# Step 0 of a gated attention: two tiles' keys on GpSimd, two pairs' masks on ScalarE and GpSimd, new places for the later steps

## The chip, the cores and the metric

The kernel runs on one core of one Trainium2 chip. The metric is the device time of one execution in microseconds. Three runs of the kernel before took 467.12, 467.70 and 467.71 us, so the median is 467.7 us.

## What is computed

A gated linear attention over 4 sequences of 768 steps with 8 heads of 48 channels, and then a two-layer network on its output:

```python
f = sigmoid(f_logit)
for t in range(768):
    state = f[t][:, None] * state + outer(k[t], v[t])      # per sequence and head, 48x48
    y[t] = q[t] @ state
h = y @ w_in                                               # 384 -> 2048
g = where(h >= 1, h, where(h <= -1, 0, (h + 1) ** 2 / 4))
out = g @ w_out                                            # 2048 -> 384
```

The large products run in a reduced format with a high and a low part for each operand, three products for each.

## The kernel before

**Steps and units.** Time is cut into six steps of 128. The attention of a step is made by blocks: the gates' running products scale keys and queries, keys times queries give a block of scores, a triangular mask cuts it, and the masked scores times the values give the step's output. From step 1 on the state of the steps before is added. The network of a step is 16 units (96 in all). A unit is 9 matrix products of 512 columns into `ph` (L317, for unit 0 L960), an activation of five instructions on ScalarE and VectorE (L320, L323, L328, L331, L334), and 9 products of 512 columns into `po` (L341).

**Step 0.** The heads lie in three tiles of 128 partitions (`m` = 0, 1, 2). `gate(m)` makes one tile's keys and queries: a sigmoid on ScalarE (L542, L544), a backward scan into `w` on VectorE (L546, s1), a copy of its ends by GpSimd (L550), a reciprocal (L552, rc), a forward scan (L553, s2), then keys times `w` (L556, km) and queries times the second scan (L558, qm). All of these after the sigmoid are on VectorE except L550 and two tiny GpSimd instructions (L563, L565). Tiles 0 and 2 go in two halves of two sequences. The scans' second operands are the constant tiles `least_w` and `rec` in SBUF. `w` is one buffer: the next tile's first scan waits until the keys of the tile before have read it.

TensorE then makes scores of four pairs of heads (L638 for pairs 0, 1 and 2, L668 for the last pair, which is put together from slices of all three tiles, so that it is complete only after tile 2). Eight masks (L681, `masks`) multiply a score bank by the mask on VectorE. `heads` (L917) and `thirds` (L932) make step 0's output from the masked scores, `rounded` (L761, L762) splits it in a high and a low part, and unit 0 begins.

**The order.** `Plan` holds every instruction group with an engine, a cost from the table `COST` and what it depends on. A list scheduler fixes each engine's order before the kernel is built; on the chip each engine works through its queue in that order and waits on semaphores. TensorE's groups stay in the order in which they are added: `START` gives it for step 0; `TURNS` and `VISITS` say beside which unit the later steps' transposes and attention stand (for each pair of pairs four places: scores, state sums, begin, output; several at one place make one stretch of TensorE's work). Where the scheduler expects a gap on TensorE in the first 20 us it puts products of zeros there (L396). `LOOK` names the engines on which the scheduler lets an instruction wait for a much more urgent one that is nearly ready.

Of the kernel before, what the change touches and what calls it, by code (L numbers as in the profile page):

```python
# [19 lines left out]
ALU = mybir.AluOpType  # L20
PSUM = bass.MemoryType.PSUM

B, H, S, D = 4, 8, 768, 48
C = 128
# [28 lines left out]
LATENCY = dict(PE=235, ACT=140, DVE=110, POOL=150)  # L53
COST = dict(mm=227, narrow=120, scores=1000, scores_half=500, heads=960, thirds=1020, half=330, both=940, begin=430, before=880, part=450, states=700, before_half=440, parts=730, parts_last=730, zeros=4000, turn=395, first=160, last=200,
            rows=316, turned_rows=150, scan=1140, dve=602, small=200, sums=467, gate=600, act=575, bits=660, round=485, copy=520, turned=412, sig=538, decay=226,
            issue=480, near=600, least=300)


INSTRUCTIONS = dict(scores=32, scores_half=16, heads=32, thirds=32, both=128, begin=64, before=128, before_half=64, part=64, states=64, parts=128, parts_last=64, zeros=24, turn=8)
BLOCK, FIRST_BLOCK, AHEAD, BEHIND, FETCH, OFFSET, WAITS = 256, 193, 48, 40, 3700, 9, 1.0045  # L60


LOOK, MARGIN, GAP = ("ACT", "DVE"), 100, 3000

SOONER = 2000
GATHER_BEHIND, GATHER_LATER = (0, 0, 0), 6000

TURNS = {4: 6.5, 6: 9.5, 8: 15.5, 10: 22.5, 12: 25.5, 14: 41.0, 16: 44.0, 18: 52.0, 20: 60.0, 22: 69.0}
VISITS = {4: (8.0, 8.0, 11.0, 11.0), 6: (11.0, 12.5, 12.5, 12.5), 8: (21.0, 21.0, 22.0, 22.0), 10: (25.0, 25.0, 28.5, 28.5), 12: (28.5, 34, 36.0, 36.0), 14: (36.0, 42.5, 42.5, 42.5), 16: (49.0, 49.0, 55.0, 55.0), 18: (54.0, 55.0, 57.0, 57.0), 20: (66.0, 66.0, 75.0, 75.0), 22: (75.0, 77, 77, 77)}
HOMES = [(k + 3) % 5 for k in range(25)]  # L70
START = (("scores", 0), ("mask", 0, 0), ("mask", 0, 1), ("last", 0), ("scores", 1), ("mask", 1, 0), ("mask", 1, 1), ("last", 1),
         ("scores", 2, 0), ("last", 2, 0), ("scores", 2, 1), ("last", 2, 1), ("first", 0), ("first", 1),
         ("mask", 2, 1), ("mask", 3, 1), ("mask", 2, 0), ("mask", 3, 0), ("second", 0), ("second", 1), ("second", 2), ("second", 3))
AFTER = {1: (('turn', 0), ('turn', 1), ('turn', 2)), 4.5: (('states', 0), ('states', 2)), 2: (('turn', 3),)}

# [23 lines left out]
class Plan:  # L99
# [7 lines left out]
    def add(self, engine, cost, emit, *deps, kb=0, count=None):  # L107
        flat, made = [], count is not None

        def spread(d):  # L110
            if isinstance(d, list):
                for e in d:
                    spread(e)
            elif d is not None and d not in flat:
                flat.append(d)

        spread(list(deps))
        cost, kind = COST[cost] if isinstance(cost, str) else cost, cost
        count = count or INSTRUCTIONS.get(kind) or 2 * max(1, round(cost / (COST["mm"] if cost % COST["mm"] == 0 else COST["narrow"])))
        if engine == "PE":  # L120
            if self.tensor is not None and self.tensor not in flat:
                flat.append(self.tensor)
            small = made or kind in SMALL_PRODUCTS
            cost += (COST["last"] if small else COST["first"]) if small != self.small else 0
            self.small = small
        o = Op(engine, cost, emit, flat, kb)
        if engine == "PE":
            o.count = count
        for d in flat:
            d.users.append(o)  # L130
        if engine == "PE":
            self.tensor = o
        self.ops.append(o)
        return o
# [96 lines left out]
def gla_moe(ctx: ExitStack, tc: tile.TileContext, ff, kqd, f0, vv, vad, vbd, wd, fixedd, gates, values, headsd, out):  # L231
    nc = tc.nc
# [46 lines left out]
    def wide(a):  # L279
        return a.rearrange("r b c -> r (b c)")  # L280
# [70 lines left out]
    add = plan.add  # L351

    def dma(dst, src, kb, *deps):
        return add("SP", "issue", lambda: nc.sync.dma_start(dst, src), *deps, kb=kb)
# [4 lines left out]
    def vec(cost, fn, *deps):  # L359
        return add("DVE", cost, fn, *deps)  # L360

    def sca(cost, fn, *deps):
        return add("ACT", cost, fn, *deps)
# [7 lines left out]
    def fresh(t):  # L371
        nc.gpsimd.memset(t, 0.0)

    def start_least():
        nc.vector.memset(least_w, 1e-30)
        nc.vector.memset(least_w[:, :, 0], 1.0)


    set_kq = add("POOL", 1500, lambda: nc.gpsimd.memset(kq[NP - 1], 0.0))
    set_least = vec(400, start_least)  # L380
    set_rec = add("POOL", 800, lambda: fresh(rec))
    set_ds = add("POOL", 200, lambda: fresh(ds[0][:, 2 * B * D:]))

# [126 lines left out]
    def old(n, *names, of=att):  # L510

        return [] if n < 0 else [of[n].get(k) for k in names]

    def gate(m):

        i, p = divmod(m, NT)
        t = kq[p]

        ft, before = (f[m], None) if m < 2 else (act_f[1], None) if m == 2 else (f[(m - 1) % 2], m - 3 if m < 5 else m - 2)
        et = end[m % 2]  # L520
        steps = ((0, 2), (2, 4)) if m in (0, 2) else ((0, 4),)
        count = len(steps)
        c = gates_of[m] = {k: [] for k in ("km", "qm", "sg", "en", "s1", "s2")}
        lk = c["lk"] = dma(t[:, 0:2 * N], kqd[i, p], 512, old(NP * (i - 1) + p, "sc", "y", "tr"),
                           old(m - NT, "km", "qm", "to", of=gates_of))
        if m == 0:
            ready["mask"] = ready["mask_t"] = ready["ident"] = dma(fixed, fixedd, 160)
            ready["f0"] = sca(200, lambda: nc.scalar.activation(f0s[:, 0:NI * NT * B], f0s[:, 0:NI * NT * B], AF.Sigmoid), dma(f0s, f0, 36))
        for h, (b0, b1) in enumerate(steps):
            cols = slice(b0 * C + (1 if b0 else 0), b1 * C + 1)  # L530
            if m != 2:
                l = dma(ft[:, cols], ff[i, p, :, cols], 256 // count, gates_of[before]["qm"] if before is not None else None)
            elif h == 0:
                l = dma(ft[:, 0:N + 1], ff[i, p, :, 0:N + 1], 256)
                l.early = SOONER
            last = old(m - 1, "km", "en", "s2", of=gates_of)
            u0, u1 = B - b1, B - b0
            fwd = ft[:, b0 * C:b1 * C]
            bwd = ft[:, b1 * C:b0 * C:-1]
            kt, qt = wide(part(t, 0)[:, u0:u1]), wide(part(t, 1)[:, b0:b1])  # L540
            if m != 2:
                sg = sca("sig" if count == 1 else 308, lambda cols=cols: nc.scalar.activation(ft[:, cols], ft[:, cols], AF.Sigmoid), l)  # L542
            elif h == 0:
                sg = sca("sig", lambda: nc.scalar.activation(ft[:, 0:N + 1], ft[:, 0:N + 1], AF.Sigmoid), l)  # L544

            s1 = vec(COST["scan"] if count == 1 else 602, lambda bwd=bwd, u0=u0, u1=u1: nc.vector.tensor_tensor_scan(  # L546
                out=wide(w[:, u0:u1]), data0=bwd, data1=wide(least_w[:, u0:u1]), initial=0.0,
                op0=ALU.mult, op1=ALU.max), sg, c["sg"], set_least, last)
            last_w = w[:, u1 - 1:(u0 - 1 if u0 else None):-1, C - 1]
            en = add("POOL", "least", lambda b0=b0, b1=b1, last_w=last_w: nc.gpsimd.tensor_copy(  # L550
                out=et[:, b0:b1], in_=last_w), s1, old(m - 2, "pf", of=gates_of))
            rc = vec("small", lambda b0=b0, b1=b1, last_w=last_w: nc.vector.reciprocal(out=rec[:, b0:b1, 0], in_=last_w), s1, last, set_rec)  # L552
            s2 = vec(COST["scan"] if count == 1 else 602, lambda fwd=fwd, b0=b0, b1=b1: nc.vector.tensor_tensor_scan(  # L553
                out=fwd, data0=fwd, data1=wide(rec[:, b0:b1]), initial=0.0, op0=ALU.mult, op1=ALU.add), rc, s1, c["s1"])
            c["s1"].append(s1)
            km = vec(COST["gate"] if count == 1 else 335, lambda kt=kt, u0=u0, u1=u1: nc.vector.tensor_tensor(  # L556
                out=kt, in0=kt, in1=wide(w[:, u0:u1]), op=ALU.mult), s1, lk)
            qm = vec(COST["gate"] if count == 1 else 335, lambda qt=qt, fwd=fwd: nc.vector.tensor_tensor(  # L558
                out=qt, in0=qt, in1=fwd, op=ALU.mult), s2, lk)
            for name, d in (("sg", sg), ("en", en), ("km", km), ("qm", qm), ("s2", s2)):  # L560
                c[name].append(d)
        to, f0m = whole(t), f0s[:, m * B:m * B + B]
        o = add("POOL", "least", lambda: nc.gpsimd.tensor_tensor(out=to, in0=et, in1=f0m, op=ALU.mult),  # L563
                c["en"], ready["f0"], c["lk"], old(NP * (i - 1) + p, "db"))
        c["pf"] = [o, add("POOL", "least", lambda: nc.gpsimd.tensor_copy(out=f0m, in_=to), o)]  # L565

    va = sd[:, 0:4 * B * 64].rearrange("u (b h e) -> u b h e", b=B, h=4)
    vb = v_all[:, 0:B * 384].rearrange("u (b e) -> u b e", b=B)
# [105 lines left out]
    def masks(n, h):  # L674

        c = att[n]
        c.setdefault("am", [None, None])
        b, ps, _ = c["held"][h]
        t = am_of[n][h]
        free = {(2, 0): lambda: att[0]["ys"][0], (3, 0): lambda: att[0]["ys"][1], (3, 1): lambda: att[3]["pt"][1]}.get((n, h), lambda: None)  # L680
        o = vec("dve", lambda: nc.vector.tensor_tensor(  # L681
            out=t, in0=ps, in1=mask.rearrange("u (o t) -> u o t", o=1).broadcast_to([C, B, C]), op=ALU.mult),
            c["sc"], ready["mask"], free())
        banks[b][:] = [o]
        c["am"][h] = o
# [628 lines left out]
```

## Time and profile before

| | us |
|---|---|
| median of three runs | 467.7 |
| span of the profiled execution, first to last instruction | 465.4 |
| what lies around that span, against the median | 2.3 |
| TensorE busy in the span | 460.2 |
| VectorE / ScalarE / GpSimd busy | 368.9 / 268.5 / 25.3 |
| start of unit 0 on TensorE | 23.18 |
| end of the last product | 461.28 |

The page gives the span of the profiled execution and no separate time for it; the table sets the span beside the median. Busy matrix products overlap and their ends are modelled, so starts of matmuls are the safer reading: in the steady part they lie 0.227 us apart.

### The profile page before, as it was taken

The page shows a single profiled execution, that of the slowest core. Times are in us where ns is not written, and L with a number is a line of the kernel's source. Part 1 is how long each engine was busy: PE and PEld are TensorE (multiplying, and loading weights), DVE is VectorE, ACT ScalarE, POOL GpSimd, SP SyncE. Part 2 cuts the span into 40 slices and gives each one's busy share as a digit, 9 for nine tenths or more (in the row PEclk, how much of TensorE's full clock was granted, in tenths as well). Part 3 has the DMA queues.
Part 4 walks back from the last instruction along what each step waited for, and adds up shares of the span by engine and source line. Part 5 has one row for each costly group of instructions (what it writes and reads, how often), then busy time and mean ns, then how long its engine had stood idle before and what let it go on. Part 6 is the DMA issues. An engine that isn't in the chain of part 4 may idle for free.

```text
span 465.4 us, 10974 instructions
## 1 busy us (share of the span) xinstructions
PE 460.2 (99%) x4551; PEld 378.2 (81%) x4551; DVE 368.9 (79%) x709; ACT 268.5 (58%) x502; POOL 25.3 (5%) x67
## 2 busy tenths in 40 slices
PE   9999999999999999999999999999999999999996
PEld 4888888888888888888888888888888888888885
DVE  7999998899999999888889987867665565655633
ACT  4599999765565646546547344556445544554443
POOL 4100110000002000002001000000000000000000
PEclk9999999999999999999999999999999999999999
DMA  8897855271050252031424016603402323434101
GB/s 293 324 330 279 296 177 170 78 216 51 3 159 1 54 130 85 28 116 48 127 56 125 25 47 200 174 2 75 142 1 86 98 78 94 159 104 123 45 0 72
DMA packets 20308, 54.35 MB, mean 117 GB/s; under 512 B 3328, under 2 KB 3968, under 8 KB 20256
## 3 DMA queue, kind: packets, MB, share of 16 engines
q1 hardware_dynamic: 20256, 53.63, 36.7%
q8 instruction: 36, 0.59, 0.5%
q14 instruction: 16, 0.13, 0.1%
HBM read 44.77 MB, written 4.72 MB: 106 GB/s over the span
## 4 chain that ended last, share of the span: by engine, by line
PE 99%; DVE 0%; ACT 0%; issue 0%; DVEq 0%
PE po L341 43%; PE ph L317 42%; PE pa L777 2%; PE ph L396 2%; PE pa L808 2%; PE ph L716 2%; PE pa L884 1%; PE pa L742 1%; PE ph L668 1%; PE ph L960 0%; PE pa L716 0%; PE pa L932 0%; PE pa L917 0%; PE po L638 0%; PE pa L863 0%; PE ph L884 0%
## 5 line engine op out<-in xcount | busy, mean ns | idle before, releaser
L317 PE MATMUL ph<-x,w_hi 128*128 128x512 f32 x570 | 145.4, 391 | 0.0
L320 ACT ACTIVATE act<-ph,half 128x512 f32<-128x512 f32 x96 | 66.0, 687 | 108.6 <-PE ph L317 108.3
L317 PEld LDWEIGHTS ph<-x,w_hi 128*128 128x128 f32 x570 | 106.6, 188 | 22.2
L328 DVE SCALAR_TENSOR_TENSOR act<-ph,act 128x512 f32<-128x512 f32 x96 | 66.1, 688 | 44.3 <-ACT act L323 43.2
L331 ACT CAST ghi<-act 128x512 fp32r<-128x512 f32 x96 | 59.5, 620 | 60.8 <-DVE act L328 60.4
L341 PE MATMUL po<-ghi,w_hi 128*128 128x512 f32 x287 | 84.3, 396 | 0.0
L341 PE MATMUL po<-ghi,w_lo 128*128 128x512 f32 x287 | 82.6, 390 | 0.0
L341 PE MATMUL po<-glo,w_hi 128*128 128x512 f32 x287 | 82.6, 390 | 0.0
L334 DVE TENSOR_TENSOR glo<-act,ghi 128x512 fp32r<-128x512 f32 x96 | 66.2, 689 | 18.5 <-ACT ghi L331 16.1
L317 PE MATMUL ph<-x,w_lo 128*128 128x512 f32 x285 | 80.1, 389 | 0.0
L756 DVE STREAM_TRANSPOSE kn<-kq 32x128 f32<-32x128 f32 x224 | 67.8, 303 | 3.6
L341 PEld LDWEIGHTS po<-ghi,w_lo 128*128 128x128 f32 x287 | 53.9, 188 | 11.4
L341 PEld LDWEIGHTS po<-glo,w_hi 128*128 128x128 f32 x287 | 53.9, 188 | 11.3
L317 PEld LDWEIGHTS ph<-x,w_lo 128*128 128x128 f32 x285 | 53.5, 188 | 11.2
L323 ACT ACTIVATE act<-act 128x512 f32<-128x512 f32 x96 | 60.7, 632 | 2.7
L341 PEld LDWEIGHTS po<-ghi,w_hi 128*128 128x128 f32 x287 | 52.7, 188 | 10.9
L469 DVE TENSOR_REDUCE ok<-raw 128x1 f32<-128x512 f32 x48 | 31.4, 680 | 13.6 <-DMA raw<-in_w 13.6
L550 POOL COPY end<-w 128x4 f32<-128x4 f32 (+1 forms) x20 | 7.1, 357 | 282.9 <-DVE w L546 242.9
L546 DVE TENSOR_TENSOR_SCAN w<-f,least_w 128x512 f32<-128x512 f32 (+1 forms) x18 | 20.7, 1157 | 2.0 <-ACT f L542 2.0
L553 DVE TENSOR_TENSOR_SCAN f<-f,rec 128x512 f32<-128x512 f32 (+1 forms) x18 | 20.7, 1156 | 0.1
L457 DVE TENSOR_TENSOR w_lo<-bits,w_hi 128x512 fp32r<-128x512 f32 (+1 forms) x25 | 16.1, 662 | 0.2
L456 ACT CAST w_hi<-bits 128x512 fp32r<-128x512 f32 (+1 forms) x25 | 14.5, 598 | 0.8 <-DVE bits L452 0.8
(138 smaller groups left out, 396.2 us busy)
## 6 DMA issues: line engine op xcount, KB each, us to landing
kq<-in_kq SPq DMA_DIRECT2D x18, 512.0 KB, 4.4
raw<-in_w SPq DMA_DIRECT2D x18, 512.0 KB, 3.6
raw<-in_w SPq DMA_DIRECT2D x14, 511.6 KB, 5.2
out_y<-raw SPq DMA_DIRECT2D x17, 256.0 KB, 2.5
f<-in_f SPq DMA_DIRECT2D x16, 256.5 KB, 2.9
v<-in_v SPq DMA_DIRECT2D x10, 384.0 KB, 4.6
raw_late<-in_w SPq DMA_DIRECT2D x7, 511.6 KB, 4.8
raw<-in_w SPq DMA_DIRECT2D x12, 256.0 KB, 3.8
```

The costliest lines, as they stand in the source:

```text
L317: nc.tensor.matmul(ps[:, to], w_in(w_hi if high else w_lo, j, kt), xt[:, kt, t, c], start=(n == 0), stop=(n == 8))
L320: nc.scalar.activation(a, ps, AF.Relu, bias=half, scale=0.5)
L323: nc.scalar.activation(a, a, AF.Square)
L328: nc.vector.scalar_tensor_tensor(out=a, in0=ps, scalar=1.0, in1=a, op0=ALU.max, op1=ALU.min)
L331: nc.scalar.copy(hi, a)
L334: nc.vector.tensor_tensor(out=lo, in0=a, in1=hi.bitcast(F32), op=ALU.subtract)
L341: nc.tensor.matmul(po[e][:, c], w_out(part, j, e), g[:, of], start=(j == 0 and n == 0 and c.start == 0), stop=(j == NJ - 1 and n == 2))
L457: l = vec(COST["dve"] * n // W, lambda: nc.vector.tensor_tensor(out=lo, in0=whole_val, in1=hi.bitcast(F32), op=ALU.subtract), h)
L469: seen.append(vec("dve", lambda z=z, op=op: nc.vector.tensor_reduce(out=ok[:, 1 + NG + z + c:2 + NG + z + c], in_=words_of(raw[2])[1].bitc ...
L546: s1 = vec(COST["scan"] if count == 1 else 602, lambda bwd=bwd, u0=u0, u1=u1: nc.vector.tensor_tensor_scan(out=wide(w[:, u0:u1]), data0=bw ...
L553: s2 = vec(COST["scan"] if count == 1 else 602, lambda fwd=fwd, b0=b0, b1=b1: nc.vector.tensor_tensor_scan(out=fwd, data0=fwd, data1=wide( ...
L756: nc.vector.transpose(kn[n % 2][u:u + 32, ::-1, r:r + 32], src[:, :, u:u + 32])
```

## The change

In step 0 alone:

- For tiles 0 and 1 the scans' second operands lie in two PSUM banks (`early`), which VectorE fills at the start by three more memsets. Tile 2 and the later steps keep `least_w` and `rec` in SBUF.
- For tiles 0 and 1 the keys' product (L556) is done by GpSimd. The first scan of tile 1 waits for the keys of tile 0 as before (they are now on another engine), and by a new dependency for tile 0's queries too.
- The four masks of pairs 0 and 1 are a copy of the score bank to SBUF by ScalarE and then an `affine_select` in place by GpSimd, in place of one VectorE product each. The four masks of pairs 2 and 3 stay on VectorE.
- `START` puts the first `heads` group between the two halves of tile 2's scores.
- `LOOK` takes in GpSimd, and four costs are set: `least`, `pf`, `select`, `keys`.
- `TURNS` and `VISITS` are new. 16 different places of attention stand in `VISITS` where there were 17: the scores (54), state sums (55) of the second half of step 4 and the output of its first half (55) come together at 57.

```diff
-            issue=480, near=600, least=300)
+            issue=480, near=600, least=400, pf=620, select=850, keys=1100)
-LOOK, MARGIN, GAP = ("ACT", "DVE"), 100, 3000
+LOOK, MARGIN, GAP = ("ACT", "DVE", "POOL"), 100, 3000
-TURNS = {4: 6.5, 6: 9.5, 8: 15.5, 10: 22.5, 12: 25.5, 14: 41.0, 16: 44.0, 18: 52.0, 20: 60.0, 22: 69.0}
-VISITS = {4: (8.0, 8.0, 11.0, 11.0), 6: (11.0, 12.5, 12.5, 12.5), 8: (21.0, 21.0, 22.0, 22.0), 10: (25.0, 25.0, 28.5, 28.5), 12: (28.5, 34, 36.0, 36.0), 14: (36.0, 42.5, 42.5, 42.5), 16: (49.0, 49.0, 55.0, 55.0), 18: (54.0, 55.0, 57.0, 57.0), 20: (66.0, 66.0, 75.0, 75.0), 22: (75.0, 77, 77, 77)}
+TURNS = {4: 6.5, 6: 10.5, 8: 17.0, 10: 22.5, 12: 27.0, 14: 40.0, 16: 43.0, 18: 53.0, 20: 65.0, 22: 75.5}
+VISITS = {4: (7.0, 7.0, 11.0, 11.0), 6: (11.0, 12.5, 12.5, 12.5), 8: (20.0, 20.0, 21.0, 21.0), 10: (25.0, 25.0, 28.5, 28.5), 12: (28.5, 33, 37.0, 37.0), 14: (37.0, 42.0, 42.0, 42.0), 16: (47.0, 47.0, 57.0, 57.0), 18: (57.0, 57.0, 58.0, 58.0), 20: (67.0, 67.0, 73.5, 73.5), 22: (73.5, 76.0, 76.0, 76.0)}
 START = (...
-         ("scores", 2, 0), ("last", 2, 0), ("scores", 2, 1), ("last", 2, 1), ("first", 0), ("first", 1),
+         ("scores", 2, 0), ("last", 2, 0), ("first", 0), ("scores", 2, 1), ("last", 2, 1), ("first", 1),
...
+    early = pa[2], po[0].rearrange("p (b c) -> p b c", b=B)
+    set_early = [vec(600, lambda: start_least(early[0])), vec(500, lambda: nc.vector.memset(early[1], 0.0))]
...
+        leasts, recs = early if m < 2 else (least_w, rec)
-            last = old(m - 1, "km", "en", "s2", of=gates_of)
+            last = old(m - 1, "km", "en", "s2", *["qm"] * (m == 1), of=gates_of)
             s1 = vec(...
-                out=wide(w[:, u0:u1]), data0=bwd, data1=wide(least_w[:, u0:u1]), initial=0.0,
+                out=wide(w[:, u0:u1]), data0=bwd, data1=wide(leasts[:, u0:u1]), initial=0.0,
             s2 = vec(...
-                out=fwd, data0=fwd, data1=wide(rec[:, b0:b1]), initial=0.0, op0=ALU.mult, op1=ALU.add), rc, s1, c["s1"])
+                out=fwd, data0=fwd, data1=wide(recs[:, b0:b1]), initial=0.0, op0=ALU.mult, op1=ALU.add), rc, s1, c["s1"])
-            km = vec(COST["gate"] if count == 1 else 335, lambda kt=kt, u0=u0, u1=u1: nc.vector.tensor_tensor(
+            by, cost, half_cost = (nc.gpsimd, "keys", 600) if m < 2 else (nc.vector, "gate", 335)
+            km = add("POOL" if m < 2 else "DVE", COST[cost] if count == 1 else half_cost, lambda by=by, kt=kt, u0=u0, u1=u1: by.tensor_tensor(
                 out=kt, in0=kt, in1=wide(w[:, u0:u1]), op=ALU.mult), s1, lk)
...
+        if n < 2:
+            o = sca("copy", lambda: nc.scalar.copy(wide(t), wide(ps)), c["sc"])
+            banks[b][:] = [o]
+            c["am"][h] = add("POOL", "select", lambda: nc.gpsimd.affine_select(
+                out=t, in_=t, pattern=[[0, B], [1, C]], compare_op=ALU.is_ge, fill=0.0, base=1 - C, channel_multiplier=1), o)
+            return
```

## Rows read from the trace of the kernel before

**Rows 1.** The page: the chain that ended last, by engine.
```profile
PE 99%; DVE 0%; ACT 0%; issue 0%; DVEq 0%
```

**Rows 2.** Stretches: length, busy PE, PEld, DVE, ACT, POOL, granted clock, DMA share, GB/s.
```profile
1.70:3.44 1.74, 1.74 (x5) 0.60 (x4) 0.00 (x2) 0.82 (x2) 0.71 (x2) 1.00 0.81 198
...
7.44:15.31 7.87, 7.87 (x88) 5.33 (x87) 7.84 (x16) 2.84 (x6) 4.24 (x9) 1.00 1.03 412
```

**Rows 3.** TensorE in order of time, step 0: start, us, what, count.
```profile
9.34 1.16 PE L638 MATMUL pa<-kq 48*128 48x128 f32 x16
...
12.75 0.27 PE L638 MATMUL pa<-kq 48*128 48x128 f32 x1
...
13.85 1.04 PE L396 MATMUL ph<-zeros 128*128 128x512 bf16 x4
14.82 0.37 PE L638 MATMUL po<-kq 48*128 48x128 f32 x1
...
23.18 0.48 PE L960 MATMUL ph<-x,w_lo 128*128 128x512 f32 x1
```

**Rows 4.** VectorE in order of time, gates of tiles 1 and 2; columns as rows 3.
```profile
7.44 1.23 DVE L546 TENSOR_TENSOR_SCAN w<-f,least_w 128x512 f32<-128x512 f32 x1 [0.31 <-ACT f L542]
8.58 0.40 DVE L558 TENSOR_TENSOR kq<-kq,f 128x256 f32<-128x256 f32 x1
8.90 0.17 DVE L552 RECIPROCAL rec<-w 128x4 f32<-128x4 f32 x1
...
10.25 0.67 DVE L556 TENSOR_TENSOR kq<-kq,w 128x512 f32<-128x512 f32 x1
10.83 0.68 DVE L558 TENSOR_TENSOR kq<-kq,f 128x512 f32<-128x512 f32 x1
11.43 1.26 DVE L546 TENSOR_TENSOR_SCAN w<-act,least_w 128x256 f32<-128x256 f32 x2
...
13.73 0.41 DVE L558 TENSOR_TENSOR kq<-kq,act 128x256 f32<-128x256 f32 x1
```

**Rows 5.** From issue to landing, the first keys' load, issued at 1.76 us.
```profile
DMA to landing us min/median/max: 4.2/4.2/4.2
```

**Rows 6.** GpSimd in order of time: one tiny copy, twice.
```profile
47.81 1.00 POOL L565 COPY f0s<-kq 128x4 f32<-128x4 f32 x1
...
95.52 0.19 POOL L565 COPY f0s<-kq 128x4 f32<-128x4 f32 x1
```

**Rows 7.** VectorE in order of time, beside those two copies.
```profile
47.61 1.22 DVE L553 TENSOR_TENSOR_SCAN f<-f,rec 128x512 f32<-128x512 f32 x1
...
95.09 0.69 DVE L328 SCALAR_TENSOR_TENSOR act<-ph,act 128x512 f32<-128x512 f32 x1
```

**Rows 8.** Groups: line, engine, operation, shapes, count, busy us, mean ns.
```profile
L726 ACT COPY am<-pa 128x512 f32<-128x512 f32 x5 | 2.8, 566 | 0.0
...
L379 POOL MEMSET kq<- 128x1028 f32 x1 | 1.0, 954 | 0.0
...
L372 POOL MEMSET rec<- 128x512 f32 x1 | 0.5, 524 | 0.4 <-POOLq L1305 0.4
```

**Rows 9.** TensorE around two stretches of attention: scores with states; scores alone.
```profile
252.16 0.84 PE L317 MATMUL ph<-x,w_lo 128*128 128x512 f32 x3
...
254.74 0.97 PE L341 MATMUL po<-ghi,w_hi 128*128 128x512 f32 x3
...
274.59 0.84 PE L317 MATMUL ph<-x,w_lo 128*128 128x512 f32 x3
...
276.46 0.97 PE L341 MATMUL po<-ghi,w_hi 128*128 128x512 f32 x3
```

**Rows 10.** Stretches after the last product; columns as in rows 2.
```profile
461.30:463.20 1.90, 0.00 (x0) 0.00 (x0) 0.61 (x2) 0.37 (x1) 0.00 (x0) 1.00 0.93 353
463.21:465.30 2.09, 0.00 (x0) 0.00 (x0) 0.00 (x0) 0.00 (x0) 0.00 (x0) 0.50 0.22 74
```

**Rows 11.** Products of zeros in the first 5.5 us: ns min/median/max, first and last start.
```profile
L396 PE MATMUL ph<-zeros x11: 607/634/635, 1.1 to 5.3; 128*128 128x512 bf16 x11
```

More of the change, by code (lines that the diff above doesn't have):

```diff
@@ L372, in fresh, with start_least @@
         nc.gpsimd.memset(t, 0.0)
-    def start_least():
-        nc.vector.memset(least_w, 1e-30)
-        nc.vector.memset(least_w[:, :, 0], 1.0)
+    def start_least(t):
+        nc.vector.memset(t, 1e-30)
+        nc.vector.memset(t[:, :, 0], 1.0)
+    early = pa[2], po[0].rearrange("p (b c) -> p b c", b=B)
+    set_early = [vec(600, lambda: start_least(early[0])), vec(500, lambda: nc.vector.memset(early[1], 0.0))]
     set_kq = add("POOL", 1500, lambda: nc.gpsimd.memset(kq[NP - 1], 0.0))
-    set_least = vec(400, start_least)
+    set_least = vec(400, lambda: start_least(least_w))
     set_rec = add("POOL", 800, lambda: fresh(rec))
@@ L546, in gate @@
             s1 = vec(COST["scan"] if count == 1 else 602, lambda bwd=bwd, u0=u0, u1=u1: nc.vector.tensor_tensor_scan(
-                out=wide(w[:, u0:u1]), data0=bwd, data1=wide(least_w[:, u0:u1]), initial=0.0,
-                op0=ALU.mult, op1=ALU.max), sg, c["sg"], set_least, last)
+                out=wide(w[:, u0:u1]), data0=bwd, data1=wide(leasts[:, u0:u1]), initial=0.0,
+                op0=ALU.mult, op1=ALU.max), sg, c["sg"], set_early if m < 2 else set_least, last)
             last_w = w[:, u1 - 1:(u0 - 1 if u0 else None):-1, C - 1]
@@ L551, in gate @@
                 out=et[:, b0:b1], in_=last_w), s1, old(m - 2, "pf", of=gates_of))
-            rc = vec("small", lambda b0=b0, b1=b1, last_w=last_w: nc.vector.reciprocal(out=rec[:, b0:b1, 0], in_=last_w), s1, last, set_rec)
+            rc = vec("small", lambda b0=b0, b1=b1, last_w=last_w: nc.vector.reciprocal(out=recs[:, b0:b1, 0], in_=last_w), s1, last, set_early if m < 2 else set_rec)
             s2 = vec(COST["scan"] if count == 1 else 602, lambda fwd=fwd, b0=b0, b1=b1: nc.vector.tensor_tensor_scan(
-                out=fwd, data0=fwd, data1=wide(rec[:, b0:b1]), initial=0.0, op0=ALU.mult, op1=ALU.add), rc, s1, c["s1"])
+                out=fwd, data0=fwd, data1=wide(recs[:, b0:b1]), initial=0.0, op0=ALU.mult, op1=ALU.add), rc, s1, c["s1"])
             c["s1"].append(s1)
-            km = vec(COST["gate"] if count == 1 else 335, lambda kt=kt, u0=u0, u1=u1: nc.vector.tensor_tensor(
+            by, cost, half_cost = (nc.gpsimd, "keys", 600) if m < 2 else (nc.vector, "gate", 335)
+            km = add("POOL" if m < 2 else "DVE", COST[cost] if count == 1 else half_cost, lambda by=by, kt=kt, u0=u0, u1=u1: by.tensor_tensor(
                 out=kt, in0=kt, in1=wide(w[:, u0:u1]), op=ALU.mult), s1, lk)
@@ L562, in gate @@
         to, f0m = whole(t), f0s[:, m * B:m * B + B]
-        o = add("POOL", "least", lambda: nc.gpsimd.tensor_tensor(out=to, in0=et, in1=f0m, op=ALU.mult),
+        o = add("POOL", "pf", lambda: nc.gpsimd.tensor_tensor(out=to, in0=et, in1=f0m, op=ALU.mult),
                 c["en"], ready["f0"], c["lk"], old(NP * (i - 1) + p, "db"))
-        c["pf"] = [o, add("POOL", "least", lambda: nc.gpsimd.tensor_copy(out=f0m, in_=to), o)]
+        c["pf"] = [o, add("POOL", "pf", lambda: nc.gpsimd.tensor_copy(out=f0m, in_=to), o)]
     va = sd[:, 0:4 * B * 64].rearrange("u (b h e) -> u b h e", b=B, h=4)
```

## The prediction

> **What bounds the kernel now.** I read the page's chain first: TensorE alone makes 99% of it [rows 1], so time can only be won where TensorE's queue holds something other than products that must be done, or by making the products cost less. Then TensorE in order of time [rows 3]. Unit 0 starts at 23.18 us, and from there to the last product the starts of matmuls have no hole, only a short toll at each change between units and attention. So the front end, up to 23.18, is what can move, and behind it everything moves along.
>
> In the front end the other engines are read by stretch [rows 2]: from 7.44 to 15.31 VectorE is busy for 7.84 of 7.87 us, ScalarE for 2.84. VectorE's queue is what TensorE waits for there: four products of zeros stand at 13.85, and the first half of tile 2's scores starts at 14.82, although its queries, made from 13.73 on, end at 14.14 [rows 3, 4]. From 14.82 on TensorE's products up to unit 0 follow each other: 23.18 - 14.82 = 8.36 us. The change reorders these 8.36 us (one `heads` group goes between the score halves) and leaves none out. So unit 0 moves by as much as tile 2's first queries move, less the 0.7 us of zeros and latency in front of 14.82, plus any new hole in the 8.36.
>
> **VectorE without the keys.** The keys of tile 0 need their load, issued at 1.76 and landed 4.2 us later, at 6.0 [rows 5]. Tile 1's first scan starts at 7.44, having waited for its sigmoid and so for its load [rows 4]: nothing done earlier on VectorE can bring it forward. From there to tile 2's first scan are 11.43 - 7.44 = 3.99 us. The change puts tile 0's second queries ahead of it (8.90 - 8.58 = 0.32) and takes the keys out (10.83 - 10.25 = 0.58), so 3.99 - 0.90 = 3.09 us are left [rows 4]. From tile 2's first scan to its first queries' end nothing is taken out: 14.14 - 11.43 = 2.71.
>
> The new memsets cost nothing: VectorE has 1.74 us without work before the first scan [rows 2], and three memsets of 512 columns at about 0.5 each (GpSimd's one took 524 ns [rows 8]) fit in; without that cover they would cost 0.5 each. For scans with an operand in PSUM no row exists. The nearest is the VectorE instruction of 512 columns that reads PSUM and took 0.69, against 0.67 for one with all in SBUF [rows 7, 4]; I take 0, and at most 0.1 for each of two full scans' lengths, 0.4 in all; a gain is excluded, since a scan's length of 1.22 is twice that of a product of the same columns and so isn't set by its reads.
>
> **GpSimd's prices.** No row has GpSimd on 512 columns with an operand. From its memsets a column costs (954 - 524)/516 = 0.83 ns, and a tiny copy 0.19 us [rows 8, 6]. One pass over 512 columns is then 0.19 + 0.43 = 0.62; bottom 0.52 (the memset itself), top two passes, 1.04. The select reads one operand: I take 0.62. The keys read two: 1.04 for a whole tile, 0.62 for a half, bottom 0.52 and 0.31.
>
> The Trainium skill (GPSIMD Engine Reference, "Performance versus the Vector engine") gives 4497 ns for a two-operand product of 2048 columns, by which a whole tile would be an estimated 1.1 us, and the sum would be the same within 0.1.
>
> **Who holds the port.** The decisive reading is a copy of 4 columns on GpSimd. Beside a VectorE scan with both operands in SBUF it took 1.00 us and ended with the scan (47.81 + 1.00 = 48.81; the scan ends at 48.83). Beside a product that reads PSUM and one SBUF operand it took 0.19 [rows 6, 7]. So one of the two engines is shut out as long as the other reads two SBUF operands, and GpSimd gets in where one VectorE instruction ends and the next begins. That a long GpSimd instruction shuts VectorE out in the same way is in no row, since no long one reads here; bounds for it are nothing and its whole length. I take the whole length, because one shared way that is exclusive for one engine is most simply so for the other.
>
> The Trainium skill says so outright (SBUF — State Buffer, "Who interferes with whom"): a VectorE instruction with two SBUF inputs and a GpSimd instruction that reads SBUF exclude each other, whoever comes first has the pair for its whole instruction. This trace shows the one half of it, the 1.00 against 0.19; by the rule the sum is the one below, without its second half that of rival 1.
>
> **The sum.** Tile 0: at 6.0 two halves of keys (GpSimd) and of queries (VectorE, two SBUF operands) are ready and take turns: 2 x 0.62 + 2 x 0.32 = 1.88, so tile 1's scan, which now waits for both engines, starts at 7.9 instead of 7.44: +0.5. Queued behind that wait is all of VectorE's gate work. Tile 1: its keys run beside a scan with an operand in PSUM and cost nothing; if they were late by 0.5, tile 2's scan would be too, as it waits for `w`. Tile 2's first scan: 7.9 + 3.1 = 11.0 instead of 11.43.
>
> Then the selects. Scores of pair 0 are there at 10.5 and of pair 1 at 13.0 [rows 3]; a copy on ScalarE takes 0.57 [rows 8], hidden by its idle time (it is busy for a third of this stretch [rows 2]), so the four selects become ready at about 11.1, 11.7, 13.6 and 14.2. Just there VectorE runs tile 2: scans with `least_w` and `rec`, keys and queries, all with two SBUF operands. Each select gets in at an instruction's end and holds the next for 0.62. All four come before tile 2's first queries, as the first three push these past 15: 11.0 + 2.7 + 4 x 0.62 = 16.2. The first scores of tile 2 start at 16.2 instead of 14.82: +1.4, and unit 0 with them. The masks of pairs 2 and 3 (one SBUF operand) no longer queue behind four others on VectorE, 2.4 us less, but they follow scores that the 8.36 us hold back anyway, so this hides nothing and saves nothing.
>
> With three selects in the way +0.8; four at 0.52 +1.0; four at 1.04 +3.1.
>
> **The new places.** One stretch of attention goes. Scores alone take 276.46 - (274.59 + 3 x 0.227) = 1.19 us of TensorE between units; scores with states 254.74 - (252.16 + 0.68) = 1.90, half of which is 0.95 [rows 9]. The first three products behind a stretch take 0.97 instead of 0.84. So 0.24 + 0.13 = 0.37 is saved; bounds 0 and 0.5 (twice the toll). The moved transposes, loads and slices' DMAs go along with their places by half a unit to six and a half, at 18 x 0.227 = 4.1 us each; steps still have over three units between the last output and their first use, which hides them, and a late one would cost its own lateness on TensorE.
>
> Against the profiled span: 465.4 + 1.4 - 0.37 = 466.4. What lies around it, 2.3 us, stays: 468.7, against the median of 467.7.
>
> **Rivals.**
> 1. GpSimd doesn't hold VectorE. Then tile 1's scan stays at 7.44, tile 2's comes at 10.5, its queries end at 13.2, its scores start behind the pair before at about 13.6: -1.2. The masks of pairs 2 and 3 must be waited for before `thirds`, 0.3 us: -0.9 on unit 0, -0.37 with the places, 466.4. For it: no VectorE instruction in the trace is longer beside a GpSimd one. Against: those hold nothing long. It decides from the point where fewer than two selects fall on tile 2's gates.
> 2. The main case, and TensorE's clock with it. TensorE would be without work from about 13.7 to 16.2. After the last product the granted clock is 1.00 for 1.9 us of idleness and 0.50 (1.2 GHz) from 463.21 [rows 10]. At the start 11 products of zeros come 0.42 apart instead of 0.227 up to 5.3 us [rows 11]; 4.7 us at that rate lose 2.3: 471.0. Against: planned zeros may fill part of the idleness.
> 3. The edits cancel: keys and selects fall half on idle or PSUM instructions, unit 0 moves by 0 to 0.4, the places give 0.37: 467.5.
> 4. Crowding at 57 and 58. Scores of step 4's second half come at 57 and its masked scores are wanted at 58, 4.1 us later; two masks, two sums, two splits and four activations there are ten VectorE instructions of 0.58, from one start to the next as in [rows 4]: 5.8 us. Up to 1.7 us of TensorE lost; on rival 1, 468.1. Against: the scheduler takes the urgent masks first.
>
> **Chances.** Main case 0.45 (slower 0.25, same 0.18, faster 0.02), rival 1 0.30 (faster 0.23, same 0.07), rival 2 0.10 (slower), rival 3 0.10 (same 0.05, faster 0.03, slower 0.02), rival 4 0.05 (same 0.03, slower 0.02). Within 0.2% means within 0.9 us, about what a measurement of this kernel can tell from no change. Together faster 0.28, same 0.33, slower 0.39. The main case by itself spans 468.0 (three selects, 0.5 for the places) to 470.4 (selects at two passes); the range goes from 466.0, just below rival 1, to 470.5, and leaves out rival 2.
>
> **What would show it.** Right: in the new profile VectorE's queries and scans of tile 2 start 0.5 to 1 us behind the end of the instruction before, each time while a select runs; tile 1's scan starts near 7.9; unit 0 near 24.6; one place of attention less between units. Wrong: selects of over 0.5 us beside VectorE instructions of unchanged pace (rival 1), selects that wait out VectorE and come late themselves, a granted clock of 0.50 before unit 0 (rival 2), or TensorE waiting at unit 58 (rival 4).

## The result, and the profile after

The changed kernel takes 470.3 us (median of six runs, 468.73 to 471.16) against 467.5 for six runs of the kernel before beside it: ratio 1.0051, interval 1.0036 to 1.0066. It is slower by half a per cent. The profiled execution spans 468.7 us in place of 465.4, so +3.3. Each profile below is one execution: it was the slowest of its runs with old places and with costs and `LOOK` alone, and the fastest with operands back in SBUF, slices not waited for, the front end alone and tile 1's keys with narrow zeros, so lengths read from these are not medians.

The page's chain of the changed kernel answers to [rows 1]: TensorE no longer makes 99% of it, and DMA, VectorE and ScalarE have entered it.

```profile
PE 92%; DVE 4%; DMA 2%; ACT 1%; issue 1%; SPq 0%; DVEq 0%; ACTq 0%
```

The two early stretches, columns as in [rows 2]: VectorE's idle time at the start took in the new memsets (1.09 us busy), ScalarE and GpSimd work more in the second stretch, VectorE is as full as before, and TensorE is now idle for 0.7 us. Its granted clock stays at 1.00.

```profile
1.70:3.44 1.74, 1.74 (x6) 0.59 (x5) 1.09 (x4) 0.73 (x2) 0.77 (x2) 1.00 0.75 177
7.44:15.31 7.87, 7.15 (x80) 4.88 (x78) 7.77 (x14) 4.42 (x10) 4.84 (x7) 1.00 1.03 408
```

TensorE in order of time, as [rows 3]: tile 2's scores start at 15.26 (14.82 before), now with a wait for the queries where zeros stood, and unit 0 at 23.64 (23.18 before).

```profile
8.45 1.16 PE L643 MATMUL pa<-kq 48*128 48x128 f32 x16
9.54 2.12 PE L399 MATMUL ph<-zeros 128*128 128x512 bf16 x9
...
15.26 0.37 PE L643 MATMUL po<-kq 48*128 48x128 f32 x1 [0.72 <-DVE kq L563]
...
23.64 0.48 PE L971 MATMUL ph<-x,w_lo 128*128 128x512 f32 x1
```

VectorE's gates, as [rows 4] (L550 is now the first scan, L557 the second, L561 the keys, L563 the queries):

```profile
6.55 1.85 DVE L563 TENSOR_TENSOR kq<-kq,f 128x256 f32<-128x256 f32 x2
8.33 1.21 DVE L550 TENSOR_TENSOR_SCAN w<-f,pa 128x512 f32<-128x512 f32 x1
...
9.79 1.22 DVE L557 TENSOR_TENSOR_SCAN f<-f,po 128x512 f32<-128x512 f32 x1
11.04 1.10 DVE L563 TENSOR_TENSOR kq<-kq,f 128x512 f32<-128x512 f32 x1
12.07 1.69 DVE L550 TENSOR_TENSOR_SCAN w<-act,least_w 128x256 f32<-128x256 f32 x2
...
14.78 0.42 DVE L563 TENSOR_TENSOR kq<-kq,act 128x256 f32<-128x256 f32 x1
```

And GpSimd beside them:

```profile
6.52 1.60 POOL L561 TENSOR_TENSOR kq<-kq,w 128x256 f32<-128x256 f32 x2 [1.39 <-DMA kq<-in_kq]
...
9.75 1.27 POOL L561 TENSOR_TENSOR kq<-kq,w 128x512 f32<-128x512 f32 x1
10.97 1.67 POOL L689 TENSOR_SCALAR_AFFINE_SELECT am<-am 128x512 f32<-128x512 f32 x2
...
15.37 1.64 POOL L689 TENSOR_SCALAR_AFFINE_SELECT am<-am 128x512 f32<-128x512 f32 x2 [1.61 <-ACT am L687]
```

Read the two together. Where both engines read two operands from SBUF (6.5 to 8.3) the two halves' queries take 1.85, where one took 0.40 [rows 4]. Beside a scan with an operand in PSUM (9.79) nobody waits: 1.22, as in [rows 7]. When two selects come (10.97 to 12.64), tile 1's queries take 1.10 instead of 0.68 [rows 4], and the pair of scans 1.69 instead of 1.26: each select holds VectorE for 0.43.

The first keys' load, as [rows 5], issued at 1.83, took 4.6 us (the longer of the two loads issued in this window):

```profile
DMA to landing us min/median/max: 2.2/3.4/4.6
```

So the front end lost 0.46 us. The last group of products starts at 463.72, where it was 460.41 before; the other 2.85 us were lost behind unit 0, in a steady part that had no stop in it. The largest stop is near 144. TensorE (two planned products of zeros, and then a wait for the split of step 1's output, which the next stretch needs; the scheduler puts zeros behind the first 20 us too, where it expects a gap of over 0.5 us, so the plan itself had a gap here):

```profile
144.89 0.61 PE L399 MATMUL po<-zeros 128*128 128x512 bf16 x2
145.85 0.94 PE L895 MATMUL pa<-v,kn 64*48 64x48 f32 x64 [0.36 <-DVE x L773]
```

The chain of the changed kernel in that region names where it begins, a transfer of 5.40 us and a ScalarE instruction behind it:

```profile
129.59 5.40 DMA kq<-kq
...
135.10 1.01 ACT ds L619 x4
136.11 0.52 ACT f L546
136.63 0.58 ACT act L320
```

SyncE's queue shows why it took that long. Before the change the two transfers of slices were issued first, at 127.45 (2.3 us to landing), then `f`, then two loads of 512 KB and one of 384:

```profile
127.45 1.16 SPq L357 DMA_DIRECT2D kq<-kq  x2
128.66 0.57 SPq L354 DMA_DIRECT2D f<-in_f  x1
130.38 0.82 SPq L354 DMA_DIRECT2D kq<-in_kq  x2
131.24 1.29 SPq L354 DMA_DIRECT2D v<-in_v  x1
```

In the changed kernel, with step 2's places moved, the big loads go ahead and slices and `f` stand behind them; each of these now takes 5.4 us:

```profile
126.78 0.82 SPq L354 DMA_DIRECT2D kq<-in_kq  x2
127.65 0.42 SPq L354 DMA_DIRECT2D v<-in_v  x1
129.02 1.15 SPq L357 DMA_DIRECT2D kq<-kq  x2
130.22 0.58 SPq L354 DMA_DIRECT2D f<-in_f  x1
```

The decay `ds` (L619) and the sigmoid (L546) wait for them at the head of ScalarE's queue, in front of a unit's activation, and that is what holds up TensorE and VectorE:

```profile
135.10 1.01 ACT L619 ACTIVATE ds<-sd,kq 112x48 f32<-112x48 f32 x4 [1.28 <-DMA kq<-kq]
136.02 0.62 ACT L546 ACTIVATE f<-f 128x513 f32<-128x513 f32 x1
136.54 0.67 ACT L320 ACTIVATE act<-ph,half 128x512 f32<-128x512 f32 x1
```

The account of the 2.85 us, from the starts of matmuls. The stretches of attention from 56 us on sum to 39.5 us against 37.7 before. In three of them there is a stop: at 143.8 (2.93 in place of 1.81), at 161 (3.06 for 2.87) and at 298 (2.58 for 1.94), together 1.95; without these the sum is 0.17 shorter than before. The rest lies between the products of the units: 0.4 at 138.8 and 143.3, 0.5 between 400 and 440, and small pieces. The 0.5 is of the same kind on VectorE: a reduction of L472 that waits for a load of weights stands in front of a unit's activation there, and TensorE waits 0.37 and 0.34 for `ghi` behind it (427.3 and 431.6).

```profile
429.60 0.69 DVE L472 TENSOR_REDUCE ok<-raw 128x1 f32<-128x512 f32 x1 [1.67 <-DMA raw<-in_w]
430.20 0.68 DVE L328 SCALAR_TENSOR_TENSOR act<-ph,act 128x512 f32<-128x512 f32 x1
```

### The profile page after: what moved, and what is told of

Its sections match the earlier page's. It is cut to its first block, busy times and chain, and to the rows that moved or that the text cites. A ratio compares the mean times of both kernels' runs of the same rounds, so it can differ in the third digit from the quotient of the medians.

```text
span 468.7 us, 10990 instructions
## 1 busy us (share of the span) xinstructions
PE 461.8 (99%) x4551; PEld 378.0 (81%) x4551; DVE 370.1 (79%) x705; ACT 270.5 (58%) x507; POOL 26.1 (6%) x74
## 4 chain that ended last, share of the span: by engine, by line
PE 92%; DVE 4%; DMA 2%; ACT 1%; issue 1%; SPq 0%; DVEq 0%; ACTq 0%
PE po L341 41%; PE ph L317 40%; PE pa L788 2%; PE pa L819 2%; PE ph L727 2%; PE pa L895 1%; DMA kq<-kq 1%; DVE kn L767 1%; DVE w L550 1%; PE pa L753 1%; DVE f L557 1%; DVE kq L563 0%; DMA f<-in_f 0%; PE ph L971 0%; PE pa L943 0%
## 5 line engine op out<-in xcount | busy, mean ns | idle before, releaser
L472 DVE TENSOR_REDUCE ok<-raw 128x1 f32<-128x512 f32 x48 | 31.7, 681 | 20.8 <-DMA raw<-in_w 20.6
L554 POOL COPY end<-w 128x4 f32<-128x4 f32 (+1 forms) x20 | 5.4, 271 | 290.6 <-DVE w L550 263.0
L557 DVE TENSOR_TENSOR_SCAN f<-f,rec 128x512 f32<-128x512 f32 x15 | 18.3, 1219 | 0.0
L550 DVE TENSOR_TENSOR_SCAN w<-f,least_w 128x512 f32<-128x512 f32 x15 | 18.2, 1216 | 0.0
```

Of the source, the lines that this page charges most:

```text
L472: seen.append(vec("dve", lambda z=z, op=op: nc.vector.tensor_reduce(out=ok[:, 1 + NG + z + c:2 + NG + z + c], in_=words_of(raw[2])[1].bitc ...
```

## The experiments

Two numbers are read from each profile: the start of unit 0, and the length from there to the last group of products (the steady part). Before: 23.18 and 437.23. Changed: 23.64 and 440.08.

**Old places.** The changed kernel with the old tables:

```diff
-TURNS = {4: 6.5, 6: 10.5, 8: 17.0, ...
+TURNS = {4: 6.5, 6: 9.5, 8: 15.5, ...
-VISITS = {4: (7.0, 7.0, 11.0, 11.0), ...
+VISITS = {4: (8.0, 8.0, 11.0, 11.0), ...
```

> The changed kernel with TURNS and VISITS of the kernel before; keys, selects and START stay changed. Theory (two separate losses: unit 0 starts 0.46 us later because of the front end, and the new places cost 2.8 us in the steady part): unit 0 stays near 23.6, the steady part has no hole, 468.0 us, 2.3 us under the changed kernel. Rival (the late front end itself upsets the steady part, whatever the places): stays near 470.2, with holes on TensorE behind 100 us.

Measured: ratio 1.0105 (1.009 to 1.012), unit 0 at 23.74, steady part 440.30. The expectation failed: the old places did not bring the old steady part back. TensorE stops at 59, 69, 144 and 295 instead. The stop at 144 is not the one of the changed kernel: the slices land after 2.3 us, and four planned products of zeros stand there. At 295 the sigmoid waits 1.64 us for `f` in front of a unit's activation, as with costs and `LOOK` alone (below). About 3 us of the span come from its end, where TensorE's branch behind the last product (L1190) takes 4.14 us in this kernel and 0.39 in the changed one.

```profile
L1190 PEldq COMPARE_BRANCH  x1: 4142/4142/4142, 466.9 to 466.9; - x1
```

**New places alone.** The kernel before with the new `TURNS` and `VISITS`.

> The kernel before with the new TURNS and VISITS alone; step 0 as before. Theory (places cost 2.8 by themselves): unit 0 at 23.2, holes on TensorE near 138 to 146, 298 and 427 us, 470.3 us. Rival (the places are fitted to the changed front end and harmless without it, saving one stretch of attention): 467.1 us, no holes.

Measured: 1.0058 (1.0045 to 1.007), unit 0 at 23.32, steady part 440.43. As expected: the places alone cost all that the whole change costs, with the same stops at 138.5, 143.7 (2.93) and 298 (2.66).

**Operands back in SBUF.** As old places, but tiles 0 and 1 scan with `least_w` and `rec`:

```diff
-        leasts, recs = early if m < 2 else (least_w, rec)
+        leasts, recs = least_w, rec
```

> As e1_old_places, but tile 0's and tile 1's scans read least_w and rec in SBUF. Theory (exclusion both ways): tile 1's keys on GpSimd (1.27 us) and the forward scan of tile 1 (1.22 us) no longer run side by side, one is drawn out by the other's length, tile 2's first scan starts 1.1 to 1.2 us later, unit 0 near 24.7, 469.1 us. Rival (GpSimd holds VectorE only for its reads of a few columns at a time, and the operand's place does not matter): unit 0 near 23.6, same time as e1_old_places.

Measured: 1.0181 (1.0158 to 1.0204), unit 0 at 24.55 in place of 23.74 for old places. Tile 1's second scan on VectorE:

```profile
9.78 2.31 DVE L557 TENSOR_TENSOR_SCAN f<-f,rec 128x512 f32<-128x512 f32 x1
```

It started 0.04 behind GpSimd's keys (9.74, 1.27 long) and took 2.31 instead of 1.22: it waited them out. The Trainium skill (SBUF — State Buffer, "Who interferes with whom") states that the two exclude each other and that the first one there keeps the pair for its whole instruction; the trace agrees, with 1.09 of GpSimd's 1.27 us. The median, 475.1 us, is 2.4 above that of old places, where 1.1 was expected; 0.81 of it lies at unit 0, and the rest was not followed up.

**Selects that only write.** The changed kernel with GpSimd's `affine_select` replaced:

```diff
-            c["am"][h] = add("POOL", "select", lambda: nc.gpsimd.affine_select(...
+            c["am"][h] = add("POOL", "select", lambda: nc.gpsimd.memset(t, 0.0), o)
```

> The changed kernel with GpSimd's four selects replaced by memsets that only write the same tiles (left out: the masks of pairs 0 and 1). Theory, exclusion is between VectorE with two SBUF operands and a GpSimd instruction that reads SBUF: the queries of tile 1 take 0.68 in place of 1.10, the first scan of tile 2 1.26 in place of 1.69 for two, the scores of tile 2 start at 14.6 to 14.9 in place of 15.26 and unit 0 at 23.0 to 23.3 in place of 23.64. Rival, any GpSimd instruction on SBUF holds VectorE: 1.10 and 1.69 stay, unit 0 at 23.5 or later.

VectorE in this kernel:

```profile
10.74 0.69 DVE L563 TENSOR_TENSOR kq<-kq,f 128x512 f32<-128x512 f32 x1
11.35 1.26 DVE L550 TENSOR_TENSOR_SCAN w<-act,least_w 128x256 f32<-128x256 f32 x2
```

GpSimd in the same time:

```profile
10.65 0.52 POOL L689 MEMSET am<- 128x512 f32 x1
11.82 0.52 POOL L689 MEMSET am<- 128x512 f32 x1 [0.65 <-ACT am L687]
```

As expected: 0.69 and 1.26, with unit 0 at 22.95 (one execution). By these two instructions, what holds VectorE is that GpSimd reads, not that it is busy. At unit 0 the selects cost less than on VectorE: it comes 16.73 us after GpSimd's first keys here (6.22 to 22.95) and 17.12 with selects (6.52 to 23.64), so 0.39; the other 0.30 is an earlier load.

**Tile 1's keys alone.** Old places, old `START`, masks and tile 0's keys on VectorE; `COST` and `LOOK` as changed:

```diff
-        by, cost, half_cost = (nc.gpsimd, "keys", 600) if m < 2 else (nc.vector, "gate", 335)
+        by, cost, half_cost = (nc.gpsimd, "keys", 600) if m == 1 else (nc.vector, "gate", 335)
-        if n < 2:
+        if n < 0:
```

> Old places, old START, all masks and tile 0's keys on VectorE; only tile 1's keys on GpSimd, beside scans with operands in PSUM. Theory (GpSimd and VectorE exclude each other only where VectorE reads two SBUF operands, so these keys are free): VectorE's queue for tile 2 comes 0.5 us earlier than before, unit 0 near 22.7, 467.0 us. Rival (keys of 1.27 us on GpSimd end after the scan and hold tile 2's first scan, and the planned zeros take the rest): unit 0 at 23.2, 467.5 us.

Measured: 1.0006 (0.9996 to 1.0016), unit 0 at 23.12, steady part 438.64. VectorE's queries came 0.47 earlier, but planned zeros kept the scores at 15.09, and 1.4 us were lost at 161 and 293. At 293 TensorE waits for a ScalarE instruction that stands behind the sigmoid, which waits for `f`:

```profile
293.24 0.63 ACT L546 ACTIVATE f<-f 128x513 f32<-128x513 f32 x1 [0.77 <-DMA f<-in_f]
293.78 0.67 ACT L320 ACTIVATE act<-ph,half 128x512 f32<-128x512 f32 x1
294.35 0.14 ACT L799 COPY seen_y<-ph 1x8 f32<-1x8 f32 x1
```

**Costs and LOOK alone.** The kernel before with nothing but these (the two GpSimd instructions L563 and L565 go by the cost `pf` from then on, in every step):

```diff
-issue=480, near=600, least=300)
+issue=480, near=600, least=400, pf=620, ...)
-LOOK, MARGIN, GAP = ("ACT", "DVE"), 100, 3000
+LOOK, MARGIN, GAP = ("ACT", "DVE", "POOL"), 100, 3000
```

> The kernel before with nothing changed but the four costs (least, pf) and GpSimd in LOOK. Theory: these alone open holes as in the version with tile 1's keys: stretches of 3.2 at 159 and 2.9 to 3.1 at 292 in place of 2.9 and 1.9, 468.7 to 469.4. Rival: they matter only together with work on GpSimd; 467.7 as before, within 0.3.

Measured: 1.0031 (1.0013 to 1.0048), with unit 0 where it was (23.18). Edits that move no work to another engine cost 1.5 us of the median (by the interval 0.6 to 2.2), at the places foreseen (the stretch at 159 takes 3.23). So the change does not lie in step 0 alone, as I wrote ahead of the prediction. Which of the edits does it was not separated. In the profiled execution the stop near 293 is the longest of all (the stretch takes 4.37), and behind 2.21 us without work TensorE's granted clock is 0.53 (windows, columns as [rows 2]):

```profile
292.00:294.00 2.00, 1.77 (x98) 1.41 (x96) 1.98 (x3) 0.42 (x1) 0.47 (x1) 1.00 0.27 87
294.00:296.40 2.40, 0.42 (x28) 0.42 (x32) 0.89 (x3) 1.71 (x4) 0.00 (x0) 1.00 0.00 2
296.50:300.10 3.60, 3.60 (x20) 2.84 (x9) 3.44 (x8) 2.78 (x10) 0.00 (x0) 0.53 0.54 171
```

Its ScalarE queue has the order of the fence above, with a longer wait:

```profile
294.69 0.63 ACT L542 ACTIVATE f<-f 128x513 f32<-128x513 f32 x1 [2.27 <-DMA f<-in_f]
295.22 0.67 ACT L320 ACTIVATE act<-ph,half 128x512 f32<-128x512 f32 x1
295.79 0.14 ACT L788 COPY seen_y<-ph 1x8 f32<-1x8 f32 x1
```

In the kernel before, the unit's activation and the small copy stand ahead of the sigmoid, and the same kind of load, 4.5 us long there too, disturbs nobody:

```profile
292.01 0.66 ACT L320 ACTIVATE act<-ph,half 128x512 f32<-128x512 f32 x1
292.58 0.14 ACT L788 COPY seen_y<-ph 1x8 f32<-1x8 f32 x1
...
293.32 0.63 ACT L542 ACTIVATE f<-f 128x513 f32<-128x513 f32 x1
```

**Slices not waited for.** The changed kernel, every engine's order untouched:

```diff
-scale=whole(kq[p])[:R, b:b + 1]
+scale=whole(kq[p if p < NP - 1 else 0])[:R, b:b + 1]
```

> The changed kernel with its order untouched, but the decay of the state for the last pair of heads (the ds activations) reads the decay factors of tile 0 in place of those that come with the slices (left out: the right factors for that pair). So ScalarE no longer waits there for a transfer that took 5.4 us at 129.6. Theory 1, the hole of 138 to 146 comes from that wait, which stands in ScalarE's queue ahead of a unit's activation: the step 0.49 at 138.81 falls to 0.24, the stretch from 143.79 falls from 2.93 to 2.2-2.4 (its two planned products of zeros stay), 470.3 becomes 469.4 to 469.7. Rival, VectorE is simply full up to 145: the first falls, the second stays at 2.8 or more, 470.0 to 470.3.

Measured: 1.0057 (1.004 to 1.0074). The step at 138.8 is back at its length (no stop), the stretch near 143 takes 2.60 in place of 2.93. That lies between the two expectations. The median did not fall (1.0057, with 1.0051 for the changed kernel); in this profile the stretch at 298 was longer (2.98). So the run shows where the wait for the slices goes, some 0.6 us at two places, and not that the whole time hangs on it.

**Slices and a lighter VectorE.** As the last, and:

```diff
+        few = slice(0, 256) if 16 <= k <= 29 else ALL
-        g["lo"] = vec("dve", lambda: act_lo(a, hi, lo), ...
+        g["lo"] = vec("dve", lambda: act_lo(a[:, few], hi[:, few], lo[:, few]), ...
```

> As the version that doesn't wait for the slices, and the last VectorE instruction of each unit from 16 to 29 works on 256 of its 512 columns, in the same order (left out: half of the low parts there, beside the factors). Theory: what was left of the hole at 143 (stretch 2.60, of which 0.45 are two planned products of zeros) is VectorE's own row of transposes, so the stretch falls to 2.2 to 2.3. Rival, another late transfer: it stays at 2.5 or more.

My theory fell: the stretch takes 2.73, not 2.2 to 2.3. VectorE had room and still waited, for ScalarE, whose next instruction waited for `f`, the other transfer behind the big loads:

```profile
135.04 0.64 ACT L546 ACTIVATE f<-f 128x513 f32<-128x513 f32 x1 [0.76 <-DMA f<-in_f]
```

So what is left of the stop at 143 begins with the second late transfer. It came later here than in the run before (a wait of 0.76 in place of 0.37), and that alone outweighs the 0.26 us that a lighter instruction saves. From 136.95 on VectorE has no gap until the split is done at 144.58, so its row of transposes hands the delay on in full: this one execution does not separate the two.

**Step 4's places back.** Keys 16 and 18 of `TURNS` and `VISITS` as before, the others as changed.

> The changed kernel with the places and turns of step 4 (keys 16 and 18) as before. Theory: the stop of 0.56 us inside the stretch at 298 (TensorE waits for nothing that the profile shows) comes from two dense stretches of small products within 8 us, so with the places spread again it goes and that stretch takes 1.9 to 2.0 in place of 2.58; the hole at 143.8 stays at 2.9; one place more costs 0.2 to 0.4: 469.8 to 470.1. Rival: such stops come anywhere with any order, then another stretch of the second half is 0.5 longer and the time stays at 470.3 or above.

Measured: 1.0081 (1.0056 to 1.0105), steady part 440.98. Half a miss. The stop that TensorE made without any visible wait at 299.7 went with the merge, but at 295 a stop of 1.1 us took its place, of the kind seen with costs alone (the sigmoid waits 2.0 us for `f` ahead of the activation). The rival came true as well: 470.9 us, and the stretch at 380 is 0.41 longer than before, with 0.15 us of it shown as "issue".

**The front end alone.** The changed kernel with old places, old costs and old `LOOK`.

> The changed kernel with the old places, the old costs and the old LOOK: what is left of the change is the front end alone (keys and masks on GpSimd, operands in PSUM, the new START). Theory: the holes behind unit 0 come from the costs and LOOK (in the version with old places alone) and from the places (in the changed kernel), and without both the steady part is that of before: unit 0 at 23.6 to 23.8, the last group of products 0.4 to 0.9 behind the 460.4 of before, 468.2 to 468.8 (3 us more where the branch at the end takes 4 us in place of 0.4, as with old places alone; then the last group is what counts). Rival: the front end by itself opens the holes of 143 and 292 because VectorE has its work there in another order: last group at 462.5 or later.

Measured: 1.0037 (1.0024 to 1.0051), unit 0 at 24.05, steady part 437.95, last group at 462.00. The rival's 462.5 was not reached: the stretches near 143 and 293 have their old 1.81 and 1.94. What is left, +0.87 at unit 0 and +0.72 behind it (0.4 of it at 162), is 1.6 together, above the 0.4 to 0.9 that I expected. In this order one select came ahead of tile 1's keys, and they then held VectorE's queries (1.75 instead of 0.69).

**Tile 1's keys, old costs, narrow zeros.** As tile 1's keys alone, with old costs and `LOOK`; and

```diff
-                warm(o.zeros)
+                warm(o.zeros, 13000 < o.start < 20000)
```

where the flag makes the product one column wide.

> Tile 1's keys alone on GpSimd beside a scan with an operand in PSUM, all else as before: masks and tile 0's keys on VectorE, the old START, places, costs and LOOK; and the products of zeros planned between 13 and 20 us have one column in place of 512 (their number is kept). Theory: VectorE's queries of tile 2 are 0.47 earlier, and without the zeros the scores follow at 14.3 instead of 15.1, unit 0 at 22.4 to 22.7; the holes at 159 and 292 of the version with the new costs are due to costs and LOOK and go: 466.4 to 467.0, faster than both. Rival: the holes come from the shifted front end itself: stretches of 3.2 at 159 and 3.1 at 292 as before, 467.4 to 468.0.

Measured: 0.9999 (0.9989 to 1.001). In its profile unit 0 starts at 22.59, the stretches at 159 and 291 take 2.87 and 2.19, the steady part is 437.49 and the last group starts at 460.07, 0.34 earlier than before. The mechanism went as expected and costs and `LOOK` are what opened those stops, but 0.34 us is less than the comparison can tell: no faster version was found.

**Narrow zeros alone.** The kernel before with that last edit.

> The kernel before with nothing changed but the products of zeros planned between 13 and 20 us: one column in place of 512, their number kept. Tells how much of the gain at unit 0 of the version with tile 1's keys and narrow zeros is the keys'. Theory: tile 2's queries end at 14.14, so its scores start at 14.35 to 14.45 in place of 14.82 and unit 0 at 22.7 to 22.9; 467.2 to 467.6. Rival: VectorE's masks are what TensorE waits for next, then unit 0 stays at 23.0 or later and the time at 467.7.

Measured: 1.0002 (0.9989 to 1.0015). Tile 2's scores start at 14.51 and unit 0 still at 23.49: TensorE waits for VectorE instead. Some 0.3 us are lost in front of the two `heads` groups, which wait for masks as the rival says, and 0.25 in front of the second half of tile 2's scores (15.76), which follows its queries (they end at 15.70). Counted from tile 1's first scan, which follows its load, unit 0 comes after 15.74 us in the kernel before (7.44 to 23.18), 15.74 here (7.75 to 23.49) and 15.28 with tile 1's keys on GpSimd (7.31 to 22.59): that 0.46 is the keys'. It also corrects a sentence of mine: the masks on VectorE do hold TensorE.

## Why the prediction was right in sign, too small in size, and wrong in its reasons

The predicted sum was +1.4 at unit 0 and -0.37 behind it. Measured were +0.46 and +2.85. The forecast of 468.7 was 1.6 below the median because both terms were off, in opposite directions. That 470.3 still lies in the stated range is luck: its upper end, 470.5, was set for selects of 1.04 us, and a select took 0.63.

**The turn of tile 0: right.** From the keys' arrival to tile 1's scan I had 1.9 us; it took 1.8 (6.52 to 8.33). What I had not seen is that with it the whole front end hangs on that load. In three profiles with these orders GpSimd's first keys start at 5.77, 6.19 and 6.52, and unit 0 at 22.89, 23.31 and 23.64, each time 17.12 later. By these, the front end costs anything from -0.3 to +0.5 against 23.18. The other side moves too: with the old step 0 and new places unit 0 is at 23.32.

**Tile 1's keys beside a scan in PSUM: right**, 1.22 against 2.31 with the operand in SBUF.

**Tile 2's first scan at 11.0: wrong**, 12.07. Later keys are 0.43 of it, a select that held tile 1's queries another 0.43; some 0.2 is left, where reciprocal and scans now wait for each other with nothing between them.

**The 8.36 us up to unit 0: not without a wait.** With costs and `LOOK` alone the scores of tile 2 start at 15.14 and unit 0 still at 23.18, 8.04 behind them. So 0.32 of the 8.36 was TensorE waiting for VectorE's masks, in the kernel before already (the mask for its second `heads` group ends at 17.78, and the group starts at 17.84). In the changed kernel these products take 8.38 (15.26 to 23.64), so it kept nothing of that.

**Four selects times 0.62: the mis-sized term of the front end.** A select takes 0.63 unhindered, as priced, but costs VectorE 0.43. Two came before tile 2's first queries, not four: pair 1's scores were taken from their old time, though they need tile 1's queries, which the first select had held. The second pair started at 15.37, behind these queries' end at 15.20. So 0.86 in place of 2.48, of which 0.39 reached unit 0.

**The new places: the step that failed most.** Its saving was priced nearly right: without the three stops the stretches are 0.17 us shorter (I had 0.24 for them and 0.13 for the toll). What failed is the sentence that the moved loads and transfers are hidden by three units and that a late one costs its own lateness on TensorE. Moved, the slices and `f` stand behind 1.4 MB of loads, land after 5.4 us instead of 2.3 and 3.0, and are waited for at the head of ScalarE's queue in front of a unit's activation. The places alone cost 2.6 us (467.7 to 470.3). That the order of issue makes them land late is read from the two traces; no run changed that order alone.

The parts do not add up. By medians the places alone cost 2.6 us, the front end alone 1.9, costs and `LOOK` alone 1.5, together 6.0, and the whole change 2.8; with old places and all else changed, the steady part stays at 440.30. So 2.6 is the price of the places in the kernel before. What they cost within the whole change is read from its trace, at the stop of 143 and the steps beside it (1.5 us), and is not shown by a difference of runs.

**Costs and LOOK: left out of the sum.** I listed them and gave them no term. Alone they cost 1.5 us. At 293 this is because they swap instructions in ScalarE's queue; the 0.36 at 159 was not followed up.

**The rivals.** Rival 1 is out: selects hold VectorE. Rival 2's clock did not fall before unit 0. Rival 3's cancelling is what the front end did, within its load's scatter, but the places did not give 0.37. Rival 4 named the right place, 57 and 58, with the wrong mechanism: the 0.64 us there show no wait for VectorE.

```profile
300.25 0.25 PE L819 MATMUL pa<-kq,later 48*48 48x64 f32 x1 [0.34 <-issue]
```

"issue" means that the profile shows nothing it waited for. The stop went when the merge was undone; its cause was not settled. The traces point at TensorE's own program. The page has a DMA queue for instructions:

```profile
q8 instruction: 36, 0.59, 0.5%
```

In the changed kernel, with places alone and with slices not waited for, TensorE goes on after this stop (300.25, 299.96, 298.84) 2.3 to 2.5 us after a packet of that queue began (297.71, 297.64, 296.41). No run tested it.

## What to carry to other kernels

When a change re-plans an in-order queue, price the order, not only the work: list for each engine which instructions now wait for a transfer, what that transfer stands behind, and whose activation stands behind the instruction. Read the plan's own signs too: it had two products of zeros at 144, and so a gap there, before any run. A saving of a few tenths from merged places is worth less than one such wait. And try a planner's costs alone, without the work they belong to: here they lost half as much as the whole change.

## What the runs showed that I had not expected

- A GpSimd select of 128x512 lasts 0.63 us and holds VectorE for 0.43; a memset of the same tile, 0.52 us long, holds it not at all.
- Behind a stop of 2.2 us in the steady part TensorE's granted clock was 0.53 over 3.6 us, with products 0.427 us apart (the 1.2 GHz level) in place of 0.227.
- The branch behind the last product took 4.14 and 4.20 us in two versions (old places, operands back in SBUF) and 0.39 in the others. No run here shows why.
